# Low rank, sum and mix of the first batch in two groups of columns, the larger one ahead of the last unit's inner products

## The chip, the cores and the metric

One core of a Trainium2 chip runs the program. The metric is the time of one execution in microseconds (us), as the device counts it; the median of the kernel before was 490.29 us in three runs, 489.82 to 490.84. "Span" is the profiler's time from the first to the last instruction of an execution; it is about 1.8 us shorter than that execution's time. A profile is one execution. The timed runs have no trace, but each lists its span and its mean granted TensorE clock.

In the profile, PE is TensorE's matmuls, PEld its weight loads, DVE is VectorE, ACT ScalarE, POOL GpSimd. L208 is line 208 of that kernel; the changed kernel's lines are 39 higher from the class's middle on, so L842 of before is L881 of after. `issue` as what ended a wait means that the profile shows no semaphore the engine waited for.

## The reference, cut to what matters

```python
# attention: batch 4, 8 heads, 768 steps, head size 48
f = sigmoid(f_logit)
state[t] = f[t] * state[t-1] + outer(k[t], v[t])
y[t] = q[t] @ state[t]
# the 8 heads side by side: x is (4, 768, 384)
xt = x.transpose(0, 2, 1)
h  = xt @ U @ V                    # U: 768 x 32, V: 32 x 768
u  = x + h.transpose(0, 2, 1)
out = u + maximum(u @ w_ch1, 0) @ w_ch2      # 384 -> 1536 -> 384
```

All in fp32. The low rank works along the 768 steps, so it treats every column of x (every channel of every head) by itself: columns can be done in any grouping.

## The kernel before

The attention is done in units of two heads, 96 columns of x, four units a batch. The steps of a unit are `kept`, `states`, `scan`, `scores` (products `sc`), `read` (products of the carried state, `y` with `st`) and `inner` (inner products of a chunk, `y` with `v_nat, A`, and then the copy of x). After the fourth unit of batch 0 its mixer begins: low rank, sum over the four row groups, mix and addition to x, the turns (transposes, copied to `uT`), then the first-layer products `pz`.

```python
        def low_rank():
            pm = ps_mm.tile([P, 512], F32, name="ph", tag="mm")
            for c in range(NCH):
                g = slice((c % NG) * R, (c % NG + 1) * R)
                nc.tensor.matmul(pm[g, 0:DM], lhsT=U[:, c, :], rhs=x[:, c, :],
                                 start=(c < NG), stop=(c >= NCH - NG))
            ...                                    # ScalarE copies pm to h[0]
        def added_up():
            ...                                    # h[1] = blocks^T h[0]
        def mix(t):
            ...                                    # pu = V_t^T h[1]; every second t:
                add(x[:, t - 1 : t + 1, :], x[:, t - 1 : t + 1, :], pu[0][:, :, 0:DM], ALU.add)
```

The weights arrive as 64-bit words and are converted in six operations each: two on ScalarE, three on VectorE, one on GpSimd. `loads` is the list of these conversions; the chunks of `w1` follow U and V in it. Where one stands in the program is where it stands in each engine's order.

```python
        def end():                                 # one conversion
            ...
            nc.scalar.activation(f, hi.bitcast(F32), AF.Abs)
            nc.scalar.activation(r, lo, AF.Copy, scale=2.0**-29)
            nc.vector.tensor_scalar(f, f, SMALLEST, LARGEST, ALU.max, ALU.min)
            nc.vector.tensor_scalar(y, y, 3, 0x3FFFFFFF, ALU.logical_shift_left, ALU.bitwise_and)
            nc.vector.scalar_tensor_tensor(y, hi, 0xC0000000, y, ALU.bitwise_and, ALU.bitwise_or)
            nc.gpsimd.tensor_tensor(dst.bitcast(I32), shaped(y.bitcast(I32)), shaped(r), ALU.add)
...
        for piece in rear(HP - 1, "read") + loads[:2] + rear(HP - 1, "inner") + loads[2 : early + 1]:
            piece()
        loads = loads[early + 1 :]
        m = mixer(0)
        start = m.before[:5] + m.firsts[0:1] + m.before[5:]
        idles = {1: 1, 2: 1}
        EARLY = 9
        ...
        for i, (_, piece) in enumerate(start + m.firsts[1:]):
            busy(idles.get(i, 0))                  # filler matmuls
            piece()
            if loads and i != 1:
                loads.pop(0)()                     # one weight conversion after each piece
            if i >= EARLY:
                next(second)()                     # one piece of batch 1's attention
```

`early` is the number of U's and V's conversions. TensorE's, VectorE's and ScalarE's orders are those of the program, but for additions and scans marked to go ahead.

## Time and profile before

| what | before | where it is read |
|---|---|---|
| median of 3 runs | 490.29 us | times |
| the profiled execution | 488.25 us, span 486.5 | times, page |
| TensorE busy | 469.6 us, 97% | page |
| last unit's inner products restart | 45.73 us | chain of waits |
| first `pz` starts | 55.72 us | chain of waits |
| from there to the end | 486.5 - 55.72 = 430.8 us | worked out |

The profiled execution was quicker than every timed one, by 1.6 us and more. That was passed over in the prediction and turns out to matter.

The prediction shows the lines for the first 60 us. Two later places come up below. First, of TensorE's timeline (start, busy us, group, and in brackets how long it stood idle before it and what ended that), the one long stop late in the kernel:

```profile
328.56 0.80 PE L749 MATMUL sc<-qT,kz 48*64 48x64 f32 x38 [0.76 <-issue]
```

Then two later stretches of the table by stretch (from and to, length, busy us and instructions of PE, PEld, DVE, ACT, POOL, then the clock, the DMA share, GB/s):

```profile
110.00:165.00 55.00, 55.00 (x870) 34.17 (x869) 48.42 (x62) 22.22 (x43) 2.00 (x2) 1.00 0.69 104
...
290.00:350.00 60.00, 58.98 (x1029) 53.97 (x1027) 46.89 (x84) 20.46 (x35) 0.00 (x0) 1.00 0.06 17
```

In the first TensorE works 55.00 of 55.00 us; in the second it lacks 1.02 us, most of it the stop of 0.76.

### The profile page before, as it was taken

The numbers are of one execution on the slowest core, as the hardware profiler recorded it, in microseconds if no ns is written. First come the engines' busy times: TensorE is split into PE (matmuls) and PEld (weight loads), VectorE is DVE, ScalarE is ACT, GpSimd is POOL, SyncE is SP. The second block draws the span as 40 slices with busy tenths as digits, with TensorE's granted clock in tenths as the row PEclk, the third lists the DMA queues.
The fourth block names the chain that finished last, engine by engine and source line by source line (L and its number), as shares of the span: only waits on it lengthen the run. The fifth ranks groups of instructions, "written<-read, shape, count | busy, mean of one in ns | idle before, by whom it ended". The sixth has DMA issues, their size and how long they took to land.

```text
span 486.5 us, 12681 instructions
## 1 busy us (share of the span) xinstructions
PE 469.6 (97%) x5519; PEld 400.0 (82%) x5519; DVE 356.7 (73%) x561; ACT 163.4 (34%) x307; POOL 36.4 (7%) x49
## 2 busy tenths in 40 slices
PE   7996899999999999999999999999999999999995
PEld 4775688886666568899899888889979999999995
DVE  5886989778998667656857449796896886858642
ACT  2444666664443223424231413432231312112200
POOL 3000345451000000000000000000000000000000
PEclk9999999999999999999999999999999999999999
DMA  9979986684777422424535100100000000000001
GB/s 146 159 149 177 264 214 144 160 151 64 112 108 118 92 42 29 62 35 90 64 50 86 26 34 1 27 3 20 18 2 0 34 2 16 18 1 34 0 34 38
DMA packets 158679, 34.34 MB, mean 71 GB/s; under 512 B 149206, under 2 KB 157078, under 8 KB 158614
## 3 DMA queue, kind: packets, MB, share of 16 engines
q1 hardware_dynamic: 158614, 33.44, 37.5%
q8 instruction: 45, 0.74, 0.7%
q14 instruction: 20, 0.16, 0.1%
HBM read 28.70 MB, written 4.72 MB: 69 GB/s over the span
## 4 chain that ended last, share of the span: by engine, by line
PE 91%; DMA 3%; DVE 3%; ACT 1%; issue 1%; SPq 1%; ACTq 0%; DVEq 0%
PE pw L273 26%; PE pz L219 23%; PE pp L371 11%; PE po L244 10%; PE y L824 3%; PE y L842 3%; PE ds L786 3%; PE sc L749 3%; PE pt L621 2%; PE pt L770 2%; PE idle L923 2%; PE put L207 1%; DMA late<-in_f_logit_dram 1%; PE pu L197 1%; PE ph L172 1%
## 5 line engine op out<-in xcount | busy, mean ns | idle before, releaser
L219 PE MATMUL pz<-uT,w 128*128 128x256 f32 x504 | 115.7, 383 | 0.9 <-ACT uT L208 0.9
L219 PEld LDWEIGHTS pz<-uT,w 128*128 128x128 f32 x504 | 93.4, 190 | 13.8 <-issue 1.1
L273 PE MATMUL pw<-w,z_all 128*128 128x192 f32 x216 | 37.7, 329 | 0.0
L273 PE MATMUL pw<-zw,w_raw 128*128 128x192 f32 x216 | 37.4, 327 | 0.0
L273 PEld LDWEIGHTS pw<-zw,w_raw 128*128 128x128 f32 x216 | 35.2, 190 | 0.8 <-issue 0.6
L273 PEld LDWEIGHTS pw<-w,z_all 128*128 128x128 f32 x216 | 35.0, 190 | 0.7
L655 DVE TENSOR_TENSOR_SCAN late<-fz,late 128x768 f32<-128x768 f32 x16 | 28.1, 1756 | 9.7 <-ACT fz L650 5.1
L229 ACT ACTIVATE z_all<-pz 128x512 f32<-128x512 f32 x33 | 19.7, 595 | 39.7 <-PE pz L219 39.6
L95 POOL TENSOR_TENSOR w<-w_y,w_r 128x384 int32<-128x384 int32 x24 | 30.3, 1262 | 35.1 <-DVE w_y L94 23.9
L371 PE MATMUL pp<-v_nat,late 128*128 128x128 f32 x224 | 28.8, 275 | 0.0
L673 DVE TENSOR_TENSOR_SCAN late<-fz,other 128x768 f32<-128x768 f32 x16 | 27.9, 1746 | 0.1
L371 PEld LDWEIGHTS pp<-v_nat,late 128*128 128x128 f32 x224 | 27.0, 192 | 0.0
L244 PE MATMUL po<-w,zw 128*128 128x384 f32 x72 | 25.6, 499 | 0.0
L244 PE MATMUL po<-w,z_all 128*128 128x384 f32 x72 | 25.3, 496 | 0.0
L364 ACT ACTIVATE other<-other 128x512 f32<-128x512 f32 x18 | 11.3, 631 | 40.0 <-DVE other L187 40.0
L812 ACT COPY st<-added 128x576 f32<-128x576 f32 x12 | 14.7, 1224 | 26.0 <-DVE added L807 26.0
L756 DVE TENSOR_TENSOR A<-sc,causal 128x768 f32<-128x768 f32 x16 | 15.2, 948 | 10.8 <-PE sc L749 10.8
L92 DVE TENSOR_SCALAR w_y<-w_y 128x384 f32<-128x384 f32 (+3 forms) x27 | 13.1, 485 | 10.6 <-ACT w_y L90 10.3
L244 PEld LDWEIGHTS po<-w,zw 128*128 128x128 f32 x72 | 12.9, 189 | 8.7 <-issue 1.2
L244 PEld LDWEIGHTS po<-w,z_all 128*128 128x128 f32 x72 | 13.1, 190 | 8.5 <-DVE o L187 0.6
L187 DVE TENSOR_TENSOR w_raw<-z_all 128x768 f32<-128x768 f32 x12 | 11.5, 955 | 10.6 <-ACT z_all L229 9.2
L273 PE MATMUL pw<-w,other 128*128 128x192 f32 x108 | 18.6, 327 | 0.0
(185 smaller groups left out, 827.5 us busy)
## 6 DMA issues: line engine op xcount, KB each, us to landing
w_raw<-in_moe_w_ch_dram SPq DMA_DIRECT2D x18, 384.0 KB, 4.2
out_dram<-o SPq DMA_DIRECT2D x24, 192.0 KB, 1.9
v_nat<-in_v_dram SPq DMA_DIRECT2D x16, 144.0 KB, 3.0
v_nat<-in_v_dram SPq DMA_DIRECT2D x32, 72.0 KB, 2.9
zw<-in_moe_w_ch_dram SPq DMA_DIRECT2D x6, 384.0 KB, 5.6
late<-in_f_logit_dram SPq DMA_DIRECT2D x10, 96.0 KB, 3.2
late<-in_k_dram SPq DMA_DIRECT2D x10, 96.0 KB, 2.7
late<-in_q_dram SPq DMA_DIRECT2D x10, 96.0 KB, 2.7
```

Of the source, the lines that this page charges most:

```text
L95: nc.gpsimd.tensor_tensor(dst.bitcast(I32), shaped(y.bitcast(I32)), shaped(r), ALU.add)
L219: nc.tensor.matmul(pm[:, i * 2 * P : (i + 1) * 2 * P], lhsT=w1[:, m, o : o + P], rhs=uT[a][:, m, :], start=(m == 0), stop=(m == NDC - 1))
L229: nc.scalar.activation(z[a, c][:, k : k + 2, :].rearrange("p i t -> p (i t)"), pm, AF.Relu)
L244: nc.tensor.matmul(pm, lhsT=z[a, i // NI][:, i % NI, s * P : (s + 1) * P], rhs=w2[:, i, :], start=(i == 0), stop=(i == NFC - 1))
L273: nc.tensor.matmul(pm[:, n * HM : (n + 1) * HM], lhsT=lhs[:, i, :], rhs=rhs[:, i, :], start=(i == 0), stop=(i == NI - 1))
L371: nc.tensor.matmul(pm[:, i, r * P : (r + 1) * P], lhsT=room["w"](wn)[:, r * P : (r + 1) * P], rhs=x_node(a, xn), start=((xn, wn) == of[0]) ...
L655: nc.vector.tensor_tensor_scan(backwards(X, S - 1, S), backwards(f, S, S), backwards(ends, S - 1, S), 0.0, ALU.mult, ALU.add,)
L673: nc.vector.tensor_tensor_scan(Y, f[:, 0:S], starts, 0.0, ALU.mult, ALU.add)
L749: nc.tensor.matmul(sc[part[s ^ par], par, c * C : (c + 1) * C], lhsT=T["k"][rows[par], chunk[2 * c + s]], rhs=T["q"][rows[par], chunk[2 * ...
L756: nc.vector.tensor_tensor(T["A"], sc[:, :, 0 : NBL * C].rearrange("p h (c i) -> p h c i", i=C), causal.unsqueeze(1).unsqueeze(1).broadcast ...
L786: nc.tensor.matmul(ds[par * PAD : (par + 1) * PAD, s, c * D : (c + 1) * D], lhsT=T["kb"][part[s ^ par], par, i, :], rhs=vt[part[s ^ par], ...
L812: nc.scalar.copy(st, states.rearrange(by_e, c=NCH))
```

## The change

The intent: three of the four units are finished while the last is still at work, so their 288 columns go through low rank, sum and mix during it, and only 96 columns are left for the end. In the core of the diff, `low_rank_of`, `added_up_of` and `mix_of` do the same as the old functions for a slice of columns; `mix_of` puts the products of several row chunks into one PSUM buffer and adds them in one instruction of VectorE: for the 288 columns two chunks each time (three additions of 576 elements), for the 96 four chunks and then two (additions of 384 and 192).

```diff
+        done, rest = slice(0, 2 * n * D), slice(2 * n * D, DM)
+        pieces = rear(n, "states") + rear(n - 1, "read") + rear(n, "scan") + loads[:1] + rear(n, "scores")
+        pieces += loads[1:2] + rear(n - 1, "inner") + rear(n, "read") + loads[2 : early + 1]
...
-        start = m.before[:5] + m.firsts[0:1] + m.before[5:]
-        idles = {1: 1, 2: 1}
-        EARLY = 9
+        low_rank_of, added_up_of, mix_of = m.some
+        low_rank_of(done)
+        loads[early + 1]()
+        for piece in rear(HP - 1, "inner"):
+            piece()
+        added_up_of(done)
+        low_rank_of(rest)
+        mix_of(done)
+        added_up_of(rest)
+        mix_of(rest)
+        loads = loads[early + 2 :]
+        start = m.before[3:5] + m.firsts[0:1] + m.before[5:]
+        EARLY = 6
...
-            busy(idles.get(i, 0))
             piece()
-            if loads and i != 1:
+            if loads:
                 loads.pop(0)()
```

(Cut: the three functions, and the buffers `h`, two instead of one.) Two side effects of the new loop count later: weight chunk 2 is converted behind the first turn's `uT` copy instead of ahead of it, and the last weight conversion comes one step of batch 1's attention later.

## The prediction

> **What bounds the kernel now.** I read the page's first part, then busy time by stretch, then the chain of waits between 36 and 60 us, then the timelines of ScalarE and VectorE there. The page says that this is a TensorE kernel, and gives the queue that carries instructions:
>
> ```profile
> span 486.5 us, 12681 instructions
> ...
> PE 469.6 (97%) x5519; PEld 400.0 (82%) x5519; DVE 356.7 (73%) x561; ACT 163.4 (34%) x307; POOL 36.4 (7%) x49
> ...
> q8 instruction: 45, 0.74, 0.7%
> ```
>
> By stretch (us, then busy us and instructions of PE, PEld, DVE, ACT, POOL, then clock, DMA share, GB/s):
>
> ```profile
> 40.00:47.50 7.50, 3.96 (x194) 3.47 (x186) 4.16 (x8) 2.71 (x10) 1.04 (x2) 1.00 0.95 166
> 47.50:55.70 8.20, 6.90 (x42) 3.47 (x43) 7.65 (x15) 4.89 (x12) 2.44 (x3) 1.00 1.05 218
> 65.00:110.00 45.00, 45.00 (x332) 38.84 (x331) 37.31 (x62) 27.75 (x57) 21.66 (x16) 1.00 0.73 161
> ```
>
> From 55.7 us on TensorE hardly stops (45.00 of 45.00 us in the third row); the waits that the profile lists for it after that come to 1.7 us in all (0.8, 0.6 and 0.3). So the end of the kernel moves with the start of the first-layer product of batch 0 (pz), at 55.72 us, and only the two stretches before it have room. The chain there (start us, us, what):
>
> ```profile
> 40.11 0.25 PE sc L749 x9
> 40.36 1.26 issue
> 41.62 0.73 PE sc L749 x31
> 42.34 0.70 PE y L842 x45
> 43.04 1.02 PE y L824 x44
> ...
> 44.30 0.25 PE y L842
> 44.55 1.18 issue
> 45.73 0.95 PE y L842 x47
> 46.68 0.02 issue
> 46.70 0.65 ACT x L848
> 47.35 0.14 issue
> 47.48 1.50 PE ph L172 x12
> ...
> 54.89 0.69 ACT uT L208
> 55.58 0.14 issue
> 55.72 2.83 PE pz L219 x12
> ```
>
> The last unit's reading ends at 44.06; its inner products (y L842) stop for 1.18 us in which no wait is shown, resume at 45.73, and only then come x, low rank (ph), sum, mix, turn (put), copy uT, pz: 9.99 us from 45.73 to 55.72. The timelines of ScalarE and VectorE show two things more:
>
> ```profile
> 53.86 0.58 ACT L90 ACTIVATE w_y<-zw 128x384 f32<-128x384 f32 x1 [2.89 <-DMA zw<-in_moe_w_ch_dram]
> 54.33 0.57 ACT L91 ACTIVATE w_r<-zw 128x384 int32<-128x384 uint32 x1
> 54.78 0.80 ACT L208 COPY uT<-put 128x768 f32<-128x768 f32 x1
> ...
> 52.06 2.68 DVE L187 TENSOR_TENSOR x<-x,pu 128x768 f32<-128x768 f32 x3
> ```
>
> The first turn's transposes began at 53.08; the first six took some 0.8 us, so uT could have started near 53.87. It started at 54.78, because the conversion of weight chunk 2 stood ahead of it on ScalarE and waited for its DMA until 53.86. That is 0.9 us of pure order.
>
> **What the Trainium skill says.** "Runtime: NRT & Kernel Launch", section "Instruction fetch mechanics": instructions come in blocks of 16 KiB, 256 instructions, by the sequencer's own DMA queue, and the cost of a block's edge is "mostly hidden". The trace agrees on the block (0.74 MB in 45 packets is 16.4 KB each) and not on the hiding: counting the program's TensorE instructions (two weight loads and two matmuls for an fp32 product, one pair for a transpose, semaphore waits one each), the holes at 40.36 and 44.55 lie exactly 256 instructions apart, and so, 28 blocks later, does a hole of 0.76 us at 328 us. They are block edges inside stretches of nothing but small matmuls.
>
> "TensorE: Matmul & The Clock Gate", Part 3 on packing small matmuls: products in different row or column groups of the array run at once. The trace agrees: the low rank's 12 records of 491 ns mean take 1.50 us together. The same page, Part 1: the clock falls after an idle window of about 3.4 us. The trace has holes of 1.26 and 1.18 us with the clock at 1.00 in the first row above, half idle; no longer hole is to be seen.
>
> "VectorE: DVE Perf Modes", section on the fixed extra latency: an fp32 tensor_tensor takes (N+151)/0.96 ns. For N=768 that is 957 ns; the trace has 951 for these adds. I use it for the new sizes.
>
> **The change part by part.** It takes out the two filler products around the sum (they fill waits, nothing gained on the path). It splits low rank, sum and mix into 288 columns, the three finished units, and 96, the last unit. The 288-column low rank moves between the last unit's reading and its inner products. U's and V's conversions move ahead. On ScalarE, uT now stands ahead of weight chunk 2. The orders after the first turn are the same in both programs, but for one weight conversion that comes a step later.
>
> Sizes. ScalarE copies: 479 ns for 384, 797 for 768, so 0.83 ns a column: 0.40 us for 288, 0.24 for 96. VectorE by the formula: 757 ns for 576 elements, 557 for 384, 357 for 192, each starting about 0.07 us before the previous one ends. TensorE: 384 columns in two rounds of column groups took 1.50 us, which I split into 1.33 and 0.17 of latency: 1.17 us for 288, 0.50 for 96.
>
> Path, in us of the old trace:
> The old block edge stood 2 instructions into the inner products; now it stands 2 instructions into the 288-column low rank, which has the same place in the stream. So TensorE does one of its 12 records at 44.1 and stops as before; I take 45.73 again for the restart. The move therefore does not use the hole; it puts 1.17 us ahead of the inner products. Low rank ends at 46.90, inner products (0.90) at 47.80.
> ScalarE copies h from 46.93, then converts chunk 1 (two operations, 0.45 apart) until 48.15, and only then x of the last unit: 48.15 to 48.80 instead of 47.85. The order costs 0.3 here.
> Low rank of 96 columns from 48.95 to 49.45; the sum of the 288 lies beside it (48.3), its copy ends at 49.1. Mix of 288 starts at 49.45, its first pair is done at 50.1.
> VectorE: three adds of 576 from 50.15, 0.69 apart, end at 52.25; sum and mix of the 96 lie beside them; the add of 384 from 52.15 to 52.70. The old first add ended at 53.01. The first turn needs all three 288-column adds (its PSUM buffer) and this one, 52.75.
> Two of its six transposes run before that; the rest end at 53.3, uT runs 53.35 to 54.05, pz starts at 54.2.
> Sum: 55.72 - 54.2 = 1.5 us, of which 0.9 is ScalarE's order and 0.6 is the adds that were done early, less what the low rank in front of the inner products and chunk 1 cost.
>
> The third turn's copy now stands behind chunk 4, whose DMA was awaited until 58.07: converted by 59.0, copy done at 59.8. pz needs it after 2.83 + 0.66 + 2.59 us from 54.2, at 60.3. It just fits. After that TensorE's work is the same, so 1.5 us should reach the end: 490.29 - 1.5 = 488.8.
>
> **The rivals.** (a) The hole closes, because the fetch comes sooner or the edge moves. For it: the place of the edge is counted, not measured, in the new program. Against: three of three holes fall on that count. Then low rank ends at 45.2, all is up to 1.6 us earlier still, but the third turn's copy, held to 59.8 by chunk 4's DMA, gives about 1.0 back: 487.8 to 488.3.
> (b) The split eats its gain: six more small products, four more copies and adds, each with its latency, and the last unit's x behind two additions. Then only ScalarE's order is left, or part of it: 489.4 to 490. For it: the path has ten hand-overs from one engine to another between 45.7 and 54.2, and 0.1 us more on each is 1 us.
> (c) The clock falls without the filler. Half speed for one window of 3.4 us would cost about 1.7 us: 490.5 to 492. Against it the first row above: 3.96 us busy of 7.5 and the clock stayed.
> (d) Eleven more matmuls net, 44 instructions, shift every later block edge. By my count the edge at 328 us still falls into small matmuls only, with 255 of them before it, so its 0.76 us stays, and no other edge gets such a stretch before it. At most 0.8 us either way.
>
> **Range and chances.** (b) and (d) reach up to 490.0, (a) down to 487.8; the old runs spread by 1.0 us (489.82 to 490.84). I predict 488.8 us, range 487.7 to 490.0. 2% is 9.8 us, more than the whole stretch that the change touches could give: faster 0.01, same 0.98, slower 0.01.
>
> **What would show it.** A hole of about 1.2 us or more inside the 288-column low rank, ending near 45.7 (if none: rival a). x of the last unit copied near 48.2, behind chunk 1. The first 576-element add near 50.1, the 384-element one ending near 52.7. uT right after its six transposes, ahead of chunk 2. pz at 54.2 and no new wait of TensorE before 65 us. The clock at 1.00 throughout. I am wrong if pz starts before 53.5 or after 55, or if what is won at pz isn't there at the end.

## The result, and the profile after

| | before, same job | after |
|---|---|---|
| median (lowest to highest), 4 runs each | 490.56 (489.82 to 491.03) | 488.51 us (487.32 to 488.71) |
| ratio of mean times, 95% interval | | 0.9955 (0.9933 to 0.9976) |

A ratio here is the mean time of one kernel's fast runs over that of the other's fast runs of the same rounds, so not quite the ratio of the medians quoted. All runs of this case count as fast except one of the catch-up kernel's, which is left out of its ratio.

The time is where it was predicted, 488.51 against 488.8. But the two traces do not show it: this profiled execution took 488.68 us, more than the 488.25 of the kernel before's. Its span is 486.9 us, and TensorE's busy time, 469.2 us, is 0.4 less than before. The same by stretch as shown of before:

```profile
40.00:47.50 7.50, 3.85 (x157) 3.05 (x149) 5.79 (x14) 3.32 (x11) 1.60 (x4) 1.00 0.92 157
47.50:55.70 8.20, 6.58 (x107) 4.13 (x100) 4.18 (x8) 3.41 (x9) 1.91 (x2) 1.00 0.98 210
290.00:350.00 60.00, 59.74 (x1034) 54.80 (x1033) 47.33 (x85) 20.32 (x34) 0.00 (x0) 1.00 0.06 17
110.00:165.00 55.00, 54.07 (x866) 33.50 (x866) 48.12 (x61) 22.42 (x44) 4.31 (x3) 1.00 0.72 107
```

Two late stretches changed. Between 290 and 350 us TensorE works 0.76 us more: the stop at 328 us is gone. Between 110 and 165 us it works 0.93 less: something waits there that did not. The chain of waits in the stretch of the change (start, us, what):

```profile
40.42 1.72 issue
42.13 0.73 PE sc L788 x31
...
44.56 0.36 PE ph L208
44.92 1.94 issue
46.86 1.18 PE ph L208 x11
...
48.35 0.56 ACT w_y L90
...
49.36 0.54 ACT x L887
...
49.94 0.52 PE ph L208 x12
50.46 0.71 PE pu L233 x8
...
51.20 0.76 DVE x L187
...
52.00 0.48 PE ph L217 x2
...
52.50 0.25 ACT h L218
...
53.60 0.57 DVE x L187
...
54.90 0.81 ACT uT L247
...
55.84 2.83 PE pz L258 x12
```

The 288-column low rank is stopped after one of its 12 records, as predicted, but both stops are longer in this execution than in the other trace: 1.72 and 1.94 us against 1.26 and 1.18. From the restart at 46.86 to `pz` it is 8.98 us; of before it was 9.99. So the path got 1.0 us shorter and the stops took it back, in this one execution. Most of that 1.0 is the order on ScalarE: from the first transpose to `pz` it is 2.64 us in the trace of before (53.08 to 55.72) and 1.85 to 1.86 in the four later traces of kernels without the split (e1, e3, e8, e9), none of which waits there for ScalarE. So 0.8 of the 1.0 is that wait, and 0.2 is left for the split.

The new waits, in TensorE's timeline. Of the other traces only those of e2 and e3 have them:

```profile
119.02 0.91 PE L881 MATMUL y<-v_nat,A 64*64 64x48 f32 x48 [0.30 <-ACT seen L870]
131.66 0.91 PE L881 MATMUL y<-v_nat,A 64*64 64x48 f32 x48 [0.63 <-ACT seen L870]
169.34 4.14 PE L283 MATMUL po<-w,z_all 128*128 128x384 f32 x12 [0.28 <-DVE o L187]
```

0.30, 0.63 and 0.28 are 1.2 us together.

### The profile page after: what moved, and what is told of

Read it like the earlier page. It is cut to its first block, busy times and chain, and to the rows that moved or that the text cites. A ratio compares the mean times of both kernels' runs of the same rounds, so it can differ in the third digit from the quotient of the medians.

```text
span 486.9 us, 12734 instructions
## 1 busy us (share of the span) xinstructions
PE 469.2 (96%) x5541; PEld 400.0 (82%) x5541; DVE 355.4 (73%) x563; ACT 163.2 (34%) x309; POOL 37.6 (8%) x49
## 4 chain that ended last, share of the span: by engine, by line
PE 79%; DVE 10%; DMA 3%; issue 3%; ACT 2%; SPq 2%; DVEq 0%; ACTq 0%
PE pw L312 26%; PE pz L258 23%; PE pp L410 11%; PE y L863 2%; PE pt L660 2%; PE sc L788 2%; PE ds L825 2%; PE y L881 2%; PE po L283 2%; PE idle L962 2%; PE put L246 1%; DMA late<-in_f_logit_dram 1%; DVE late L694 1%; DVE late L712 1%; PE pt L809 1%
## 5 line engine op out<-in xcount | busy, mean ns | idle before, releaser
L95 POOL TENSOR_TENSOR w<-w_y,w_r 128x384 int32<-128x384 int32 x24 | 31.5, 1311 | 41.5 <-DVE w_y L94 36.5
```

## The experiments

Four explanations of the 2 us stood open. *Path*: the split and the order on ScalarE, as predicted, 0.9 of it from the order alone. *Edges*: the stops, which fall on block edges of the instruction stream, moved, and the one at 328 us went. *Conversion*: the last weight conversion, a step later, costs 1.2 us, so the rest must have won more. *Clock*: the runs differ in the granted clock, and the two kernels' samples were unlike.

All twelve kernels were correct, and every one lies within 2% of before. "Before" is that of the same job.

| run | runs | median (range), us | before: median (runs) | ratio (95%) | mean clock of the runs |
|---|---|---|---|---|---|
| e1_before_again | 14 | 489.87 (487.52 to 493.67) | 490.13 (53) | 0.9990 (0.9965 to 1.0016) | 0.9933 |
| e2_after_again | 22 | 489.44 (487.09 to 492.78) | 490.13 | 0.9982 (0.9965 to 0.9998) | 0.9936 |
| e3_order_alone | 22 | 491.04 (488.60 to 493.33) | 490.13 | 1.0025 (1.0010 to 1.0040) | 0.9936 |
| e4_after_order_undone | 8 | 487.76 (486.99 to 489.50) | 490.13 | 0.9944 (0.9919 to 0.9968) | 0.9950 |
| e5_catch_up | 8 | 487.53 (485.75 to 493.19) | 490.18 (49) | 0.9930 (0.9900 to 0.9959) | 0.9936 |
| e6_other_bank | 21 | 487.19 (485.46 to 490.83) | 490.18 | 0.9944 (0.9925 to 0.9963) | 0.9941 |
| e7_fillers | 11 | 487.17 (486.36 to 493.39) | 490.18 | 0.9951 (0.9921 to 0.9982) | 0.9956 |
| e8_order_caught_up | 22 | 490.62 (487.09 to 492.18) | 490.18 | 0.9991 (0.9975 to 1.0007) | 0.9910 |
| e9_edges_moved | 22 | 489.74 (486.65 to 493.93) | 490.77 (29) | 0.9972 (0.9953 to 0.9990) | 0.9916 |
| e10_loads_later | 8 | 488.84 (487.76 to 491.74) | 490.77 | 0.9965 (0.9941 to 0.9989) | 0.9920 |
| e11_bank_and_edges | 6 | 487.54 (486.93 to 488.15) | 490.92 (11) | 0.9935 (0.9914 to 0.9956) | 0.9942 |
| e12_all | 6 | 487.07 (486.27 to 488.46) | 490.92 | 0.9932 (0.9909 to 0.9956) | 0.9962 |

### The same two kernels again

No edit: the kernel before, and the changed kernel.

> The kernel before, unchanged, for a second trace on the chip of the others. The first trace of before had a span of 486.5 us from a run of 488.25 us, while its timed runs took 489.8 to 491.0, and pz began there no later than in the changed kernel's trace (55.72 against 55.84 us). Theory H (the holes at the block edges differ from run to run, the first trace of before was a lucky one): here the two holes before pz sum to well over the 2.44 us of that trace and pz starts at 56.5 or later. Theory L (the gain arises after pz, not before): holes and pz as in the first trace, within 0.3 us, and the time is lost later. Ratio to before 1.000 either way.

> The changed kernel, unchanged. Ratio to before 0.9955 as at first, 2.2 us. Theory H: pz starts earlier than in e1 of the same chip by some 1.5 to 2.2 us. Theory L: pz within 0.5 us of e1's, and the difference shows in waits of TensorE after 60 us, such as the hole at 328 us, which the first trace of the changed kernel doesn't have.

With 22 runs of the changed kernel the gain is 489.34 against 490.25 in the means, 0.9 us, not 2.2. And the runs of either kernel spread over 5 us and more. The table by stretch of e1's profiled execution shows why (same columns as above, the clock is the third last):

```profile
46.00:48.00 2.00, 0.97 (x51) 0.88 (x54) 1.04 (x3) 0.85 (x3) 1.04 (x2) 0.93 0.90 172
48.00:50.00 2.00, 2.00 (x12) 0.55 (x12) 1.83 (x6) 1.11 (x3) 0.45 (x1) 0.50 1.00 168
50.00:52.00 2.00, 2.00 (x8) 0.94 (x5) 0.51 (x2) 1.25 (x3) 0.99 (x1) 0.71 0.89 171
```

The clock falls to one half and comes back: it is at half for (1 - 0.93)/0.5 x 2 = 0.28, 2.00 and (1 - 0.71)/0.5 x 2 = 1.16 us, that is 3.4 us in all. (By the same working it is 6.8 us in the traces of e6 and e9 and 10.2 in e8's, two and three times as long.) In e1's chain the low rank that took 1.50 us now takes nearly twice that, and `pz` starts later:

```profile
47.94 2.77 PE ph L172 x12
...
56.91 2.83 PE pz L219 x12
```

Of the two theories neither held as it was put: the two stops sum to 1.53 + 1.18 = 2.71 us, not well over 2.44, and `pz` is past 56.5 mainly by the clock.

In e2 it happens later, over the turn and `pz` itself:

```profile
52.00:54.00 2.00, 1.64 (x21) 1.31 (x18) 1.08 (x3) 0.12 (x1) 0.00 (x0) 0.96 1.07 329
54.00:56.00 2.00, 2.00 (x8) 1.64 (x7) 0.77 (x3) 2.00 (x4) 0.00 (x0) 0.50 1.27 197
56.00:58.00 2.00, 2.00 (x8) 1.64 (x7) 1.73 (x3) 1.15 (x3) 1.00 (x1) 0.69 1.02 263
```

Its `pz` took 3.82 us instead of 2.83. So rival (c) of the prediction is real, but it is no property of the change: the kernel before loses its clock just the same, with its filler in place. The two first traces, at 0.999 and 0.998, were both executions in which it did not happen. One such stretch takes 0.5 x 3.4 / 488 = 0.0035 off the mean clock. Over all 156 runs of the kernel before in these four jobs, the nine with a mean clock of 0.997 or more average 488.91 us and the 70 at 0.991 or less 491.30; of the changed kernel's 26 runs, nine average 487.76 and seven 491.01. What the clock does decides more than the change does.

The four changed runs of the first job had a mean clock of 0.9972, the 22 here 0.9936. A least-squares line through the 22 gives 0.7 us of time for each us of span lost to the clock (one through the 142 control runs of before gives 0.5); 0.0036 x 488 x 0.7 is 1.2 us, an estimate. That is about what lies between the first job's gain of 2.2 and this one's 0.9, though the clocks of the first job's runs of before are not on record.

### The order alone, and the order undone

The kernel before, with chunk 2 converted one piece later, so that the first `uT` copy comes first; and the changed kernel, with chunk 2 converted ahead again:

```diff
-            if loads and i != 1:
+            if loads and i not in (1, 2):
```
```diff
-        loads = loads[early + 2 :]
+        loads[early + 2]()
+        loads = loads[early + 3 :]
```

> The kernel before with one thing of the change: the conversion of weight chunk 2 comes after the first turn's copy uT on ScalarE, no split of the columns. My prediction gives 0.9 us of its 1.5 us to this: then 489.6 against 490.5 us (ratio 0.998), uT right after its six transposes. Rival: in a usual run pz's chain is so late that chunk 2's DMA has landed and been converted before uT is ready, so the order is worth under 0.3 us (ratio 0.9995 or more).

> The changed kernel with weight chunk 2 converted ahead of uT again, as before, the split kept. Prediction's account: 0.9 us of the gain is lost, ratio to before 0.9975. Rival: chunk 2 lands at 53.9 us and is converted by 54.9 us, when uT is only just ready, so nothing is lost (ratio 0.9955 as the changed kernel).

Both come out the wrong way round for the prediction. The order alone is slower, 1.0025; without it the changed kernel is at 0.9944, against e2's 0.9982. The span less the start of `pz` tells what happens later. Once the stop at 328 us, the three waits and a slow `pz` are allowed for, it hardly scatters:

| kernel | span - start of pz | us | remark |
|---|---|---|---|
| before, first trace | 486.5 - 55.72 | 430.8 | stop at 328 us of 0.76 |
| e1, before | 487.9 - 56.91 | 431.0 | stop of 0.86 |
| e3, order alone | 489.2 - 56.80 | 432.4 | stop of 1.12; waits of 0.30, 0.63, 0.27 |
| e8, order caught up | 490.4 - 59.34 | 431.1 | stop of 0.87 |
| after, first trace | 486.9 - 55.84 | 431.1 | no stop; waits of 0.30, 0.63, 0.28 |
| e2, after | 487.1 - 55.02 | 432.1 | the same; pz 1.0 longer by the clock |
| e4, after, order undone | 487.8 - 56.40 | 431.4 | no stop, no waits; pz 1.4 longer by the clock |
| e5, catch up | 486.7 - 56.80 | 429.9 | no stop, no waits |
| e6, other bank | 486.3 - 56.25 | 430.1 | no stop, no waits |

The three waits of 1.2 us come with the edit that shifts the conversions by one step (e3, the changed kernel and e2), and go when it is undone (e1, e4). How, the timelines of VectorE show. In e2:

```profile
115.80 0.36 DVE L92 TENSOR_SCALAR w_y<-w_y 128x384 f32<-128x384 f32 x1 [1.45 <-ACT w_y L90]
...
117.07 1.75 DVE L694 TENSOR_TENSOR_SCAN late<-fz,late 128x768 f32<-128x768 f32 x1
```

In e1, the kernel before:

```profile
116.29 1.76 DVE L655 TENSOR_TENSOR_SCAN late<-fz,late 128x768 f32<-128x768 f32 x1 [0.90 <-ACT fz L650]
```

In e1 the scan of the next unit waits only for its gates (`fz`). In e2 the last weight conversion lies between the gates and the scan, in ScalarE's order and in VectorE's. The scan ends later, ScalarE's copy `least` waits for it, and behind `least` stands the copy `seen` that TensorE waits for, as ScalarE's timeline in e2 shows:

```profile
118.85 0.21 ACT L699 COPY least<-late 128x12 f32<-128x12 f32 x1 [2.64 <-DVE late L694]
118.97 0.15 ACT L870 COPY seen<-y 128x2 f32<-128x2 f32 x1
```

In e4's profiled execution the order did cost what the prediction says, and more: TensorE waits for `uT` behind chunk 2, 1.93 us of this timeline (0.33 of it stands in the changed kernel too, so the order cost 1.6).

```profile
56.40 4.24 PE L258 MATMUL pz<-uT,w 128*128 128x256 f32 x12 [1.93 <-ACT uT L247]
```

Yet over eight runs e4 is the quicker kernel; its last conversion is in time again, which the next section prices at 1.2 us. In e1 chunk 2 stands ahead of `uT` as well, and costs nothing: its conversion, freed by its transfer, began at 54.81, before the first transpose at 55.05, since e1's path was late by its stops and its clock; no wait for ScalarE stands between `put` and `pz` in its chain. ScalarE's timeline in e1:

```profile
54.81 0.56 ACT L90 ACTIVATE w_y<-zw 128x384 f32<-128x384 f32 x1 [1.87 <-DMA zw<-in_moe_w_ch_dram]
...
55.97 0.80 ACT L208 COPY uT<-put 128x768 f32<-128x768 f32 x1
```

### The conversions caught up

The changed kernel with one more conversion in the loop, so that the last one comes where it did before; and the kernel before with the order alone and the same catching up:

```diff
+            if i == 5:
+                loads.pop(0)()
```
```diff
-            if loads and i != 1:
+            if loads and i not in (1, 2):
+                loads.pop(0)()
+            if i == 8:
                 loads.pop(0)()
```

> The changed kernel, but the weight conversions, which come one step late in it, catch up by one in the sixth step after the mix (two conversions in that step), so that ScalarE's and VectorE's order in batch 1 is that of before. Theory S (the step by which conversions are late costs about 1.2 us: TensorE's waits of 0.29 and 0.63 us for the small copy seen near 119 and 132 us and of 0.26 us for o near 169 us in both traces of the changed kernel and in e3, none of them in before's or e4's): those three waits are gone, time 1.0 to 1.3 us below the changed kernel's 489.44 of the same chip, near e4's 487.8, ratio to before about 0.9955. Rival (the waits are hidden again by slack later): time as the changed kernel's, ratio 0.998.

> The kernel before with uT ahead of chunk 2 as in e3, but caught up by one conversion as in e5: the order of ScalarE by itself, without the late conversions of batch 1. Theory S: about 1.2 us below e3's 491.04, that is 489.8, and none of the waits near 119, 132 and 169 us. My prediction's 0.9 us for the order: 489.2. If the order is worth nothing here, 490.1, as before.

In both the three waits are gone. e5's rest after `pz` is 429.9, which is the changed kernel's 431.1 less 1.2; e2's 432.1, less the 1.0 of its slow `pz`, agrees. So the late conversion costs 1.2 us. e8 sets the order apart from that cost: 0.9991 with an interval of ±0.0016. By that interval alone the order may be worth nothing or the predicted 0.9 us (0.9982). Runs of like clock say more: of those at 0.993 to 0.996 e8's six average 489.59 and the 23 of before in its job 489.75, while e3's 15 are 1.6 us above the 26 of before in theirs, 1.2 of which is the late conversion. So in the kernel before the order is worth little in the mean. Within the changed kernel it is open: e4 and e5 differ by it (0.9944 and 0.9930), but ran in different jobs, and their intervals overlap.

### Another PSUM buffer for the sum of the 96

The step that was off in the chain above is the sum of the last 96 columns: TensorE's timeline has it start at 52.00 after a wait of 0.35 for the addition, since it takes a buffer that the first addition empties. In e6, on top of the catching up, that sum gets a buffer from the other pool:

```diff
+            if cols.start:
+                pm = ps_mm.tile([P, 512], F32, name="ph", tag="mm")
+            else:
+                pm = ps_big.tile([P, 2, 512], F32, name="ph", tag="big")[:, 0]
```

> e5, and the sum of the last unit's 96 columns goes to a PSUM buffer of the other pool, so that it needn't wait until the first add has emptied one. In the traces of the changed kernel that wait (0.35 us), the copy after it and the mix after that make the add of 384 start 0.3 us after VectorE is free. Expected: no wait of the sum for an add, the adds run on without a gap, pz 0.3 us sooner after the restart than in e5 (8.7 instead of 9.0 us when the clock holds), ratio 0.0006 below e5's, which the timing can hardly tell. Rival: the mix still needs a buffer that the second add empties, so nothing changes.

The chain of e6:

```profile
50.73 0.53 PE ph L208 x12
51.26 0.74 PE pu L236 x8
...
52.02 2.09 DVE x L187 x3
```

The three additions now follow each other, and no sum stands between them. From the low rank of the 96 to `pz` it is 56.25 - 50.73 = 5.52 us, against 55.84 - 49.94 = 5.90 in the changed kernel: 0.4 us. In the times e6 and e5 cannot be told apart, 0.9944 and 0.9930.

### The block edges

In the kernel before alone, every filler matmul in two halves. The work is the same, but there are more instructions, so each later edge falls elsewhere:

```diff
-            for _ in range(n):
-                nc.tensor.matmul(idle[:, 0:DM], lhsT=ident, rhs=ends[:, 0:DM], start=True, stop=True)
+            for _ in range(2 * n):
+                nc.tensor.matmul(idle[:, 0 : DM // 2], lhsT=ident, rhs=ends[:, 0 : DM // 2], start=True, stop=True)
```

> The kernel before, with each filler product of 384 columns made of two of 192: the same filler work, 52 instructions more on TensorE before the dense stretch at 38 us, nothing else. Theory E (the holes without a shown wait are edges of blocks of 256 instructions): the first hole moves from the scores (sc, after 14 of its records) to the third unit's reading, after 32 of its 44 records, and the second from the last unit's inner products (after 1 record) to its reading, after 19 or 20 of 44 records. At 328 us the edge before the old hole then stands in the slow pw products, 15 instructions ahead of the small ones, nearly as in the changed kernel, where no hole is seen: the hole of 0.8 us there is gone, time 0.8 us below before (ratio 0.9984). Rival (the holes belong to those places, by a semaphore or a buffer that the trace doesn't show): holes at the same instructions as before, and the hole at 328 us stays.

TensorE's timeline of e9:

```profile
36.31 0.46 PE L749 MATMUL sc<-qT,kz 48*64 48x64 f32 x16 [0.48 <-issue]
...
43.60 0.71 PE L824 MATMUL y<-st,qT 48*64 48x48 f32 x20
45.83 0.73 PE L824 MATMUL y<-st,qT 48*64 48x48 f32 x24 [1.52 <-issue]
```

The second stop cuts the last unit's reading after 20 of 44 records, where the count puts it (19 to 20); another counted edge shows at 36.31, before the last 16 of 48 `sc`. The edge between these two, counted into the reading of the unit before, made no stop here (in e11 it does, 0.35 us, after 32 of that reading's records), and the stop at 328 us is gone. The unchanged mathematics with other edges is 0.28% (0.10 to 0.47%) quicker than before, 1.4 us in the means, of which the stop at 328 us accounts for 0.8 to 0.9; the rest is not explained. That stop goes in the changed kernel too, so some of its gain is not the split of the columns, but a shift of the instruction stream.

That the stops at the counted places are stops of the instruction fetch is an inference from these places. A test of its neighbour, the queue: e6 with the next batch's first loads issued later, behind the weight chunks.

```diff
-            elif n > 1:
-                load(n + 2, "f", "k", "q", "v")
...
+        load(HP, "f", "k", "q", "v")               # after low_rank_of(done)
+        load(HP + 1, "f", "k", "q", "v")           # after mix_of(rest)
```

> e6 with the f, k, q and v loads of units 4 and 5 (packets of 192 bytes) asked for after the first low rank and after the second mix, so that the weight chunks go ahead of them. Theory F (a block's fetch takes 4.1 us from restart to restart in e1 to e6 because its packets share the DMA engines with these loads): from the first hole's end to the second's less than 3.7 us, at the quiet place near 328 us it was about 3; second hole 0.8 us or less; clock drops fewer; time up to 1 us below e6's 487.2 if nothing waits for units 4 and 5 later. Rival: the fetch takes as long with weight chunks in the queue, 4.1 us again, and the loads now come late for the turns of unit 4 near 66 us: time as e6 or worse.

TensorE's timeline of e10:

```profile
44.51 0.93 PE L791 MATMUL sc<-qT,kz 48*64 48x64 f32 x34 [3.84 <-issue]
```

The first stop became 3.84 us (the longest otherwise is 2.22, in e11), and the second went. Nothing but the order of the transfers differs from e6, so the stops seem to depend on what the DMA queues hold at that moment; the hope that they would shrink failed. This rests on one profiled execution. At 488.84 us it is behind e6 (487.19), though not beside it in one job.

### Fillers, and all of it together

e7 is e6 with three short filler matmuls in the waits, against the clock. e11 is e6 with e9's halved fillers; e12 is e11 with e7's.

```diff
+        def short():
+            nc.tensor.matmul(idle[:, 0 : DM // 2], lhsT=ident, rhs=ends[:, 0 : DM // 2], start=True, stop=True)
         added_up_of(done)
+        short()
...
         added_up_of(rest)
+        short()
         mix_of(rest)
+        short()
```

> e6 with three short filler products (192 columns, 0.33 us each) in the waits after the first sum, the second sum and the second mix. Theory C (much of the spread between runs, 487.1 to 492.8 us, is TensorE's clock at half for about 3.4 us at a time after the idle stretch from 40 to 56 us, which e1 to e4 show at 47.9, 53.9, 47.8 and 57.8 us): mean granted clock above e6's 0.993 to 0.995, fewer runs at 0.992 or less, mean time lower although the path is up to 0.3 us longer. Rival: the idle time that matters is that of the holes at the block edges before the restart, which no filler reaches; clocks as in e6, time the same or 0.3 us more.

> e6 with the fillers in halves as in e9: the block's edge before pz now stands in the last unit's reading (after 19 or 20 of 44 records), so the 288-column low rank, whose x has long been there, is no longer cut; there is no hole at 328 us in e6 to win. e9 won 0.0012 more than the 0.8 us of the hole at 328 us, by a smaller first hole (0.5 instead of 1.3 to 2 us). Theory E: one hole of 0.5 us or less near 36 us and one of about 1.5 us in the reading, span from 0.3 to 0.8 us below e6's, ratio to before 0.9925 to 0.994. Rival: the fetch comes no sooner, the rest of the reading now has to be done after the hole as well (0.4 us), and the time is e6's, 0.9944.

> e11 with e7's three short fillers. If e7's higher mean clock (0.9956 against e6's 0.9941) was more than chance, the mean clock here is above e11's and fewer runs lie at 0.992 or less; time e11's or up to 0.5 us less. If it was chance, clocks as e11's and 0 to 0.3 us more.

e11's edge did move into the last unit's reading, as expected, but the stop there was 2.22 us, longer than the 1.5 expected; its ratio cannot be told from e6's. The clock of the filled ones is a little higher (0.9958 over 17 runs, against 0.9941 over 27 without), the time is not lower (means 487.68 and 487.48). Whether the fillers hold the clock stays open; one of e7's runs fell to 0.984 with them. e12's profiled execution has the shortest span of the profiled ones, 484.7 us, and `pz` at 53.85, 1.9 us before the kernel before's. But 484.7 - 53.85 is 430.85, a whole us more than e5's (e7, with `pz` at 53.94, loses the same: 431.2). Its chain tells where that went:

```profile
52.44 5.96 DMA zw<-in_moe_w_ch_dram
...
58.48 0.56 ACT w_y L90
...
59.49 0.07 ACT uT L250
```

The chain no longer runs over the mixer's path but over a weight transfer that lands at 58.39. The third turn's copy stands behind its conversion, and TensorE waits for that copy at 60.23 (0.31 us) and later for `z_all` at 75.06 (0.30 us). This is what the prediction said under rival (a): what comes before about 54.2 us at `pz` is given back to the weights.

e6, e11 and e12 are all below both kernels, 3.0 to 3.9 us in the medians against before; which of the three is best, these runs do not tell.

## Why the prediction was right or wrong

**The total** was right: 488.8 predicted, 488.51 in the first job and 489.44 in the larger one, both inside the range. It was right partly by luck: errors cancel, and the first job's four runs had an unusually high clock. By the prediction's own sign, `pz` after 55, its path was wrong: `pz` starts at 55.84 in the first trace and at 55.02 in e2.

**The cut of the low rank** after one record: right. The restart: not at 45.73, but at 46.86. The stops of the two first traces differ by 0.46 and 0.76 us; the prediction took the restart for a fixed time, and it varies from run to run (from 45.3 to 47.3 us in traces with the same place of the edge).

**The path after the restart**: right to 0.1 us as far as the additions. Counted from the restart: low rank's end 1.18 (1.17 predicted), the low rank of the 96 at 3.08 (3.22), the first addition at 4.34 (4.42). The mis-sized term is "sum and mix of the 96 lie beside them": the sum waited 0.35 for its PSUM buffer, and the addition of 384 began at 6.74 instead of 6.42. `pz` came 8.98 after the restart instead of 8.47; the other 0.2 are hand-overs around the turn.

**0.9 us from ScalarE's order**, as a fixed amount: the step that does not hold. It was read from one execution, in which the chunk's DMA happened to land after the turn. There it was real, 0.8 us as worked out above, but in e4's trace it was 1.6 us, in e1's nothing: it is a race between the weights and a path whose start varies by 2 us. Alone and caught up it gives 0.9991 ± 0.0016 (e8), which leaves room for anything from nothing to 1.2 us; the runs of like clock point to little.

**"One weight conversion that comes a step later"**, treated as free: wrong, it costs 1.2 us at 119, 132 and 169 us (e3, e5, e8). "After that TensorE's work is the same" overlooked that it moves into the next unit's chain on VectorE.

**Rival (d)**, "its 0.76 us stays": wrong, it went, in all variants of the changed kernel, and 0.8 us with it. The count puts 255 small instructions ahead of that edge; the edge before it comes right after slow products. That the sequencer gets ahead during these would explain it; e9, in which the edge was put among the slow products and the stop went as forecast, fits that, but no run shows it. **Rival (b)** miscounts: not six but thirteen small products are added (six of the low rank, one of the sum, six of the mix), as (d)'s eleven net of two fillers says.

**Rival (c)**: the clock does fall, in both kernels, with the filler and without; "against it the first row above" was true of that execution only.

The sum, from the traces with a held clock: path -1.0 (0.8 of it the order, in that one execution of before), stop at 328 us -0.8, late conversion +1.2, together -0.6 us instead of the -1.5. The larger job's mean gain is 0.9. Its changed kernel had 0.0016 more mean clock, which by the line above is some 0.5 us; -0.6 and -0.5 make -1.1. If the order counts for nothing, the same sum is -0.3. Both lie within the interval of ±0.8 around -0.9, so the runs do not tell which. For e6 the same terms (split -0.2, other buffer -0.4, stop -0.8, clock 0.0022 x 488 x 0.7 = -0.8) make -2.2 without the order and -3.0 with its 0.8, against -2.9 in the means, give or take 0.9: again both fit.

The higher clock is probably no accident of the samples. The 94 runs of the changed kernel and its variants have a mean clock of 0.9943, the 222 runs of kernels without the split 0.9920; 35% of the first (31% without e7 and e12, the filled ones) and 7% of the others were at 0.997 or more. Jobs and chips differ, and what in the split would hold the clock no run shows, so the cause of this part stays open, as does that of the scatter in the stops.

## What to carry to other kernels

Before a gain of one part in 500 is taken from a trace, look whether the trace is a typical execution: here the first one was quicker than every timed run, and a wait read from it was gone in the next. When the loop around a change is shifted, follow everything that the shift moves, to the last item, and not only what the change is about; the late weight conversion cost 1.2 us, more than the whole change won on its path. Split the time at a fixed landmark (here the start of `pz`): what lay behind it repeated to some 0.2 us among traces with the same stops and waits, while the whole scattered by 5.

## What the Trainium skill lacked or had wrong

- "Runtime: NRT & Kernel Launch", section "Instruction fetch mechanics": "mostly hidden" does not hold here for stretches of small matmuls; the stops at counted edges were 0.35 us (e11) to 2.22 us (e11), and 3.84 us with the weight chunks ahead in the queues (e10); that they are fetches is inferred from their places. The page does not say that the order of other DMA transfers can change a stop. The 256 instructions agree with the places in e9.
- "TensorE: Matmul & The Clock Gate", Part 1: the length of the throttled stretch, about 3.4 us, and the half clock agree (3.4 us at 0.50 in e1 and in e2; 6.8 and 10.2 us in others are two and three times that). The trigger in that part's table of two states does not: it asks for an idle window of that length, and in e2 TensorE was busy 1.64 of the 2.00 us in which the clock fell, with no stop over 1.4 us since 40 us. Further down the same page lets frequent short pauses between groups of matmuls do it, which fits better, but without a figure; no page gives the share of busy time that holds the clock.
- No page says how much the time of one and the same kernel on one core varies with this: 488.26 to 494.96 us in the 53 runs of the first four experiments' job, with mean clocks of 0.999 to 0.983.
